# A third copy of VectorE's exponentials on GpSimd, split output projections, and zero products into a free bank

## The chip, the core and the metric

The kernel runs on one core of one Trainium2 chip. The metric is device time in microseconds, the median of the runs shown; times come with a trace of one profiled execution. The engines are named as in the profile: PE is TensorE (PEld its weight loads), ACT ScalarE, DVE VectorE, POOL GpSimd, SP the engine that issues DMAs.

## The reference

Four layers on a sequence of 2048 tokens of width 512, with 32 heads of 16. Layers 0 and 2 ("A") attend causally within segments of 512 tokens and add a memory term from the segments before; layers 1 and 3 ("B") are full attention over all 2048 tokens.

```python
def _A_ref(x, wq, wk, wv, wo, beta):              # H = 32, Dh = 16, N = 4 segments, L = 512
    ...
    for s in range(N):
        logits = einsum('bhqd,bhkd->bhqk', qs, ks) * scale + mask
        a_dot = einsum('bhqk,bhkd->bhqd', softmax(logits), vs)
        pq = phi(qs)                                # phi(t) = t + 1 where t > 0, else exp(t)
        a_mem = einsum('bhld,bhde->bhle', pq, M) / (einsum('bhld,bhd->bhl', pq, z)[..., None] + 1e-06)
        outs.append(g * a_mem + (1.0 - g) * a_dot)
        M = M + einsum('bhld,bhle->bhde', phi(ks), vs); z = z + phi(ks).sum(2)
    return o @ wo

def _B_ref(x, wqkv, wo):
    scores = einsum('bhqd,bhkd->bhqk', q, k) * Dh ** (-0.5)
    return einsum('bhqk,bhkd->bhqd', softmax(scores), v) @ wo

x = x + _A_ref(_layernorm(x), ...); x = x + _B_ref(_layernorm(x), ...)     # layers 0, 1
x = x + _A_ref(_layernorm(x), ...); x = x + _B_ref(_layernorm(x), ...)     # layers 2, 3
```

Most of the work is the exponentials of the scores: with 32 heads, each B layer alone has 32 x 2048 x 2048 of them.

## The kernel before

A planner in Python (`Builder`) writes out every engine's instruction list by hand. For each instruction it keeps an estimate of the engine's time (`self.sc.t[...]`, from the `ns` and `gap` that each call gives), and picks the next piece of work by these estimates. On the chip nothing is rearranged: each engine runs its list in order and waits on semaphores where a producer is another engine, or itself.

**Units.** Attention is worked in units (`unit`, L1322). A unit multiplies keys by masked queries (`qm`) into PSUM banks of 128 keys x 512 queries; four heads stand in four row tiles of TensorE, so a product takes 32 rows (`tile=(32, 32*r, 128, 0)`). Two bank groups take turns (`SLOTS`), three banks each; ScalarE then makes one exponential of 1024 or 1536 columns from two or three banks into `pT` (L1386). Two units later (`pv_step`, `pv`) TensorE multiplies values with `pT` into an accumulation bank, 17 columns a head: 16 of values and a column of ones for the softmax sum.

**VectorE's exponentials.** In B layers the planner may give chunks of 512 columns to VectorE (`dx_open`, `ring_open`, `dx_pick`). A chunk's scores go to a bank of their own (bank 3 or 7, `misc_bank` and `sums_bank`). VectorE computes scores times a constant plus a constant into 16-bit integers whose bits, read as bf16, are a straight-line approximation of the exponential: the first step, `dx_first`, L1022, from PSUM, for one chunk (512 columns) or a pair (1024). Then `task_dx` (L1043 to 1059) adds two constants (`EXP_STEPS`, 36 and 84) to these integers, SBUF to SBUF, 1024 columns each: two copies, L1054. TensorE sums the products of all three, which evens out the approximation, so each chunk costs three products with the values where ScalarE's costs one (`pv_taken`, `pv_phase`). A chunk's buffers are `dxt` at first; when layer 0 is done (`self.wide`) those of `KA`, `QA`, `VA` and of lent weights (`wA`, `wB`) are taken too, so the same line shows in the profile under several tiles.

**Between the units.** LayerNorm, projections, the memory, output projections and the copies are tasks, generators that yield `[needs], products on TensorE, ns on VectorE`; `background` and `bg_one` run them where the estimates have room. A task that yields `["cont"]` is in the middle of a product that holds `misc_bank`; while one is, no pair of chunks opens (L942) and the two special banks are not exchanged (`can_trade`). `task_out` (L844) is the output projection: four products with `wo` in a bank and an addition to the residual (L873), in one piece. `evac` (L450) moves a projection out of PSUM on VectorE, or on ScalarE where that engine's estimate is earlier by `EVAC_ACT`.

**Other work of GpSimd.** Causal masks in `pT` (L1400), masked queries (L1293) and ones in `VB` (L803). **Zero products.** `keep_busy` (L407) adds products with a zero matrix into the open accumulation bank when TensorE's recent share of streaming falls under `FILL`, to keep its clock up.

Of the kernel before, what the change touches and what calls it, by code (L numbers as in the profile page):

```python
# [12 lines left out]
NCH = 4  # L13
# [252 lines left out]
class Builder:  # L266
# [15 lines left out]
    PART = 2  # L282
    TRADE = 100
    BACK = 5
    FILL_DVE = 300
    EARLY = 200
    FILL = 0.48
    BUSY_ROOM, BUSY_BACK = 600, 1330
    BUSY_COLS = 1024
    DVE_FIN, DX_FIN = 600, 9000  # L290
    EVAC_ACT = 500
    DX_BANK, DX_LATE, BG_BANK, DVE_LATE, DVE_LATE_LOW = 500, 800, 200, 1200, 5000
    CR_A, CR_B, CR_W, CR_LOW, CARRY, CARRY_W, REST, NEAR, SLACK = 1450, 1500, 1700, 3000, 0, 800, 14, 14, 450
    ALT3, ALT5, GAP, AHEAD, PE_B, PE_A, PE_LOW, LOW, PAIRS, TAKEN, RATE, RATE_P = 2, 4, 2, 400, 4, 2, 5, 24, 30, 0.34, 1, 1
# [112 lines left out]
    def keep_busy(self):  # L407


        g = self.cur  # L410
        cols = 32 if g is not None and g.flip else 128
        while g is not None and g.npv and self.sc.t["pe"] + self.BUSY_ROOM < self.sc.t["act"] and self.bg_cols < self.BUSY_COLS and self.sc.streamed(
                max(self.sc.t["pe"], self.sc.t["act"] - self.BUSY_BACK), 3413) < self.FILL:
            bank = g.bank
            self.mm(self.ps[0:cols, bank.col0:bank.col0 + 512], self.zero[:, 0:cols], self.woB[:, 0, :], False, False,
                    [self.b_zero, self.b_woB], bank, g.acc, tile=(128, 0, cols, 0))
            self.bg_cols += 512
# [426 lines left out]
    def task_out(self, L, s):  # L844
        isA = L % 2 == 0
        wo, bwo = (self.woA, self.b_woA) if isA else (self.woB, self.b_woB)
        for ti in range(4):
# [3 lines left out]
            if isA and ti == 0:  # L851
# [11 lines left out]
                need.append(self.later())  # L863
            yield need, 4, 700
            t = 4 * s + ti
# [3 lines left out]
            srcs = [(self.oT[:, k, c, :], c, [self.b_oT[k][c]]) for c in range(NCH)]  # L869
            for n, (a, c, ba) in enumerate(srcs):  # L870
                self.bg_cols += 512
                self.mm_wide(bank, a[:, ti * 128:(ti + 1) * 128], wo[:, c, :], n == 0, n == len(srcs) - 1, list(ba) + [bwo], al)
# [170 lines left out]
    def task_dx(self):  # L1043
        while True:
            yield ["pair"], 0, 350
            b, ents = self.dx_pairs.pop(0)
            self.dx_now = ents
            w = 512 * len(ents)
            s = self.dx_buf(b, 0)[:, 0:w]
            for k, c in enumerate(EXP_STEPS):  # L1050
                if k:
                    yield [], 0, 350
                d = self.dx_buf(b, k + 1)[:, 0:w]
                self.op("dve", (lambda d, s, c: lambda e: e.tensor_scalar(d, s, float(c), None, op0=ALU.add))(d, s, c), reads=[self.b_dxt[b][0]],  # L1054
                        writes=[self.b_dxt[b][k + 1]], ns=430 if len(ents) == 2 else 295)
            self.dx_now = []
            self.dx_use[b] = len(ents)
            for i, (g, what, r) in enumerate(ents):
                self.dxq.append((self.step + self.DX_LAG, g, what, r, b, i, [0]))
# [499 lines left out]
    def pv_taken(self, g, now, used=()):  # L1559
# [5 lines left out]
        for ent in ents:  # L1565
            _, _, what, r, slot, i, done = ent
            while done[0] <= len(EXP_STEPS) and (now or not g.flip):
                self.pv_phase(ent)
        back = sum(len(EXP_STEPS) + 1 - ent[6][0] for ent in ents)
        for level in range(1, self.LEVEL + 1):  # L1570
            if level > 1 and max(loads) < level and back - self.BACK < 0:
                break
            for ent in ents:
                if ent[6][0] <= len(EXP_STEPS) and loads[ent[3]] < level:
                    loads[ent[3]] += 1
# [45 lines left out]
    def attention(self):  # L1621
# [19 lines left out]
        self.misc_banks = [self.misc_bank.idx]  # L1641
        self.unit_no = 0
        self.parts = {}
# [123 lines left out]
```

## Time and profile before

| | us |
|---|---|
| median of 3 runs | 1788.83 (1788.11, 1788.83, 1793.23) |
| profiled execution | 1788.65 |
| its span | 1786.7 |
| busy: ScalarE | 1729.1 |
| busy: TensorE, as matmuls | 1610.9 |
| busy: VectorE | 1504.3 |
| busy: GpSimd | 124.6 |

Busy time of an engine counts overlapping instructions once. The mean of one instruction is longer than its share, because an engine starts the next before the last has ended; the distance between starts is the price of one more. Matmuls are pipelined, so TensorE's busy time says little of its room. A window of the trace gives for each engine the busy time and, after x, the count of instructions.

### The profile page before, as it was taken

To read this page: it belongs to the slowest core of one execution; us is meant where nothing else is said; L and a number is where in the kernel's file an instruction comes from. 1 tells how busy PE (TensorE), PEld (TensorE's weight loads), DVE (VectorE), ACT (ScalarE), POOL (GpSimd) and SP (SyncE) were. 2 spreads that over 40 slices of the span, in tenths; PEclk is the share of its full clock that TensorE was granted. 3 is DMA by queue.
4 is the path that set the end of the run, shared out by engine and by line. 5 is a ranking of instruction groups with operands and counts; after the bars stand their busy time and mean duration, and the time that the engine had idled before them with its cause. 6 is when DMAs were issued, how large, how long until landed. Compare 5 with 4: busy or idle time off the path is not lost.

```text
span 1786.7 us, 45990 instructions
## 1 busy us (share of the span) xinstructions
PE 1610.9 (90%) x18926; PEld 578.7 (32%) x18995; DVE 1504.3 (84%) x3202; ACT 1729.1 (97%) x1613; POOL 124.6 (7%) x228
## 2 busy tenths in 40 slices
PE   8988898888998998899899999989899889889988
PEld 5542434222234222522235222432222222222225
DVE  5757666599995998699987999748999999999996
ACT  7999999999998999899999999999999999999998
POOL 1110101110001000100001000110100000000000
PEclk9999999999999999899999999999999999999999
DMA  5211211011101111101212111120100000000000
GB/s 172 34 23 28 37 22 25 14 27 49 25 11 29 51 40 34 33 15 46 63 18 36 46 37 33 20 55 8 31 13 19 10 12 24 10 10 17 16 13 18
DMA packets 148434, 54.50 MB, mean 31 GB/s; under 512 B 128768, under 2 KB 147712, under 8 KB 148224
## 3 DMA queue, kind: packets, MB, share of 16 engines
q1 hardware_dynamic: 148224, 51.56, 13.3%
q8 instruction: 149, 2.44, 0.6%
q14 instruction: 61, 0.50, 0.1%
HBM read 18.88 MB, written 2.10 MB: 12 GB/s over the span
## 4 chain that ended last, share of the span: by engine, by line
ACT 48%; PE 25%; issue 14%; DVE 12%; DMA 1%; POOL 0%; ACTq 0%; DVEq 0%; SPq 0%; POOLq 0%
ACT pT L1386 47%; PE ps L420 25%; DVE KA L1022 2%; DVE dxt L1022 1%; DVE dxt L1054 1%; ACT amem L650 1%; DVE VB L455 1%; DVE QA L1054 1%; DVE x L873 1%; DVE VA L1054 0%; DVE lnst L558 0%; DVE xn L585 0%; DVE wA L1022 0%; DVE qm L1293 0%; DVE oT L861 0%
## 5 line engine op out<-in xcount | busy, mean ns | idle before, releaser
L1386 ACT ACTIVATE pT<-ps 128x1024 bf16<-128x1024 f32 (+1 forms) x1572 | 1700.1, 1253 | 41.2 <-PE ps L420 37.0
L420 PE MATMUL ps<-qm,KB 32*128 32x512 bf16 x4096 | 582.4, 385 | 125.3 <-ACT pT L1386 106.3
L420 PE MATMUL ps<-pT,VB 128*17 128x512 bf16 x2961 | 505.0, 385 | 0.5 <-DVE x L873 0.2
L1022 DVE TENSOR_SCALAR KA<-ps 128x512 uint16<-128x512 f32 x549 | 381.2, 698 | 12.4 <-PE ps L420 8.0
L420 PEld LDWEIGHTS ps<-qm,KB 32*128 32x128 bf16 x4096 | 153.6, 91 | 645.4 <-ACT pT L1386 543.8
L1022 DVE TENSOR_SCALAR dxt<-ps 128x512 uint16<-128x512 f32 (+1 forms) x399 | 275.6, 692 | 7.4 <-PE ps L420 4.2
L420 PE MATMUL ps<-dxt,VB 128*17 128x512 bf16 x1179 | 278.6, 382 | 0.0
L420 PEld LDWEIGHTS ps<-pT,VB 128*17 128x17 bf16 x2961 | 118.2, 87 | 290.7 <-issue 279.6
L420 PE MATMUL ps<-QA,VB 128*17 128x512 bf16 x538 | 171.2, 382 | 0.0
L1054 DVE TENSOR_SCALAR dxt<-dxt 128x1024 uint16<-128x1024 uint16 (+1 forms) x414 | 164.1, 419 | 1.3
L420 PE MATMUL ps<-VA,VB 128*17 128x512 bf16 x538 | 158.1, 382 | 0.0
L420 PE MATMUL ps<-KA,VB 128*17 128x512 bf16 x538 | 145.1, 381 | 0.0
L1293 POOL TENSOR_SCALAR qm<-QB,par 128x512 bf16<-128x512 bf16 x90 | 68.3, 762 | 781.0 <-PE ps L420 745.1
L1054 DVE TENSOR_SCALAR QA<-KA 128x1024 uint16<-128x1024 uint16 (+1 forms) x284 | 120.5, 424 | 1.9
L1054 DVE TENSOR_SCALAR VA<-KA 128x1024 uint16<-128x1024 uint16 (+1 forms) x284 | 118.1, 416 | 0.0
L420 PE MATMUL ps<-qm,KA 32*128 32x128 bf16 (+2 forms) x1536 | 93.0, 257 | 18.9 <-ACT pT L1386 13.4
L420 PE MATMUL ps<-VA,pT 128*128 128x51 bf16 (+1 forms) x2560 | 106.6, 189 | 2.0 <-DVE ob L1481 1.3
L420 PE MATMUL ps<-woB,zero 128*32 128x512 bf16 (+1 forms) x306 | 101.4, 383 | 0.2
L1400 POOL TENSOR_SCALAR_AFFINE_SELECT pT<-pT 128x256 bf16<-128x256 bf16 (+4 forms) x92 | 48.7, 544 | 748.5 <-ACT pT L1386 694.2
L420 PEld LDWEIGHTS ps<-VA,pT 128*128 128x128 bf16 x2560 | 92.6, 97 | 19.8 <-issue 8.5
L420 PE MATMUL ps<-xT,wB 128*32 128x512 bf16 (+1 forms) x747 | 74.6, 381 | 2.2 <-DVE VA L1054 0.5
L420 PE MATMUL ps<-xT,wA 128*32 128x512 bf16 (+1 forms) x524 | 68.5, 381 | 4.4 <-DMA xT<-xn 1.3
(138 smaller groups left out, 1421.3 us busy)
## 6 DMA issues: line engine op xcount, KB each, us to landing
wB<-in_B_wqkv_dram SPq DMA_DIRECT2D x48, 128.0 KB, 2.3
wA<-in_A_wk_dram SPq DMA_DIRECT2D x16, 128.0 KB, 2.2
wA<-in_A_wq_dram SPq DMA_DIRECT2D x16, 128.0 KB, 2.3
wA<-in_A_wv_dram SPq DMA_DIRECT2D x16, 128.0 KB, 2.4
out_dram<-x SPq DMA_DIRECT2D x8, 256.0 KB, 2.2
x<-in_A_x_dram SPq DMA_DIRECT2D x3, 512.0 KB, 8.1
wB<-in_B_wqkv_dram SPq DMA_DIRECT2D x1, 1536.0 KB, 11.6
oT<-ob SPq DMA_TRANSPOSE x63, 2.5
```

Source lines behind the costliest of these rows:

```text
L420: self.sc.add("pe", lambda e: e.matmul(out, lhsT, rhs, start=start, stop=stop, skip_group_check=True), reads=reads, banks=[(bank, "w", all ...
L455: self.op("dve", lambda e: e.tensor_copy(dst, src), writes=bdst, bank=bank, alloc=al, ns=690)
L650: self.op("act", lambda e: e.activation(et, src, ACT.Exp), reads=bsrc, writes=self.b_amem, ns=1023, gap=915)
L873: self.op("dve", (lambda t, o: lambda e: e.tensor_tensor(self.x[:, t, :], self.x[:, t, :], o, ALU.add))(t, o), reads=[self.b_x[t]], writes ...
L1022: self.op("dve", lambda e: e.tensor_scalar(d, o, SCALE * LOG2E * 128, 127.0 * 128 + EXP_BIAS, op0=ALU.mult, op1=ALU.add), writes=[self.b_d ...
L1054: self.op("dve", (lambda d, s, c: lambda e: e.tensor_scalar(d, s, float(c), None, op0=ALU.add))(d, s, c), reads=[self.b_dxt[b][0]], writes ...
L1293: self.op(eng, (lambda m, q, col: lambda e: e.tensor_scalar(m, q, col, 0.0, op0=ALU.mult, op1=ALU.add))(m, q, col), reads=[bq, self.b_par] ...
L1386: self.sc.add("act", (lambda dst, src: lambda e: e.activation(dst, src, ACT.Exp, scale=SCALE))(dst, src), writes=self.b_pT[slot * 3 + i:sl ...
L1400: self.op("pool", (lambda blk, pat: lambda e: e.affine_select(blk, blk, pattern=pat, compare_op=ALU.is_ge, fill=0.0, base=0, channel_multi ...
```

## The change

Four things, and constants that go with them. (1) In `task_dx`, where a chunk pair is full (1024 columns), the kernel is in its wide stage, GpSimd's estimated time is under VectorE's by the measure `POOL_COPY` and neither chunk's group is near its end, the copy with 84 goes to GpSimd, ahead of VectorE's copy with 36; both read the first step's output. (2) `pv_taken` leaves out a chunk's next product while the copy that it reads is not estimated to be ready within `DX_READY`. (3) `task_out` in the wide stage yields after its first product (four instructions) and goes on with the other three. (4) `keep_busy`, where no accumulation is open, may write zero products into the special bank that comes free first.

```diff
+    POOL_COPY, POOL_NEAR, DX_READY = 1000, 10, 300
+    OPART = 1
...
-    BUSY_ROOM, BUSY_BACK = 600, 1330
+    BUSY_ROOM, BUSY_BACK = 400, 1330
     BUSY_COLS = 1024
+    BUSY_WAIT = 200
     DVE_FIN, DX_FIN = 600, 9000
-    EVAC_ACT = 500
-    DX_BANK, DX_LATE, BG_BANK, DVE_LATE, DVE_LATE_LOW = 500, 800, 200, 1200, 5000
-    CR_A, CR_B, CR_W, CR_LOW, CARRY, CARRY_W, REST, NEAR, SLACK = 1450, 1500, 1700, 3000, 0, 800, 14, 14, 450
+    EVAC_ACT = 300
+    DX_BANK, DX_LATE, BG_BANK, DVE_LATE, DVE_LATE_LOW = 500, 900, 200, 1200, 5000
+    CR_A, CR_B, CR_W, CR_LOW, CARRY, CARRY_W, REST, NEAR, SLACK = 1450, 1500, 1700, 3000, 0, 800, 12, 12, 450
     ALT3, ALT5, GAP, AHEAD, PE_B, PE_A, PE_LOW, LOW, PAIRS, TAKEN, RATE, RATE_P = 2, 4, 2, 400, 4, 2, 5, 24, 30, 0.34, 1, 1
     NKS, DX_LAG = 6, 2
     DMA_STEPS, DMA_LATE = 1, 300
@@ -408,12 +411,18 @@
 
 
         g = self.cur
-        cols = 32 if g is not None and g.flip else 128
-        while g is not None and g.npv and self.sc.t["pe"] + self.BUSY_ROOM < self.sc.t["act"] and self.bg_cols < self.BUSY_COLS and self.sc.streamed(
+        bank, al = (g.bank, g.acc) if g is not None and g.npv else (None, None)
+        while self.sc.t["pe"] + self.BUSY_ROOM < self.sc.t["act"] and self.bg_cols < self.BUSY_COLS and self.sc.streamed(
                 max(self.sc.t["pe"], self.sc.t["act"] - self.BUSY_BACK), 3413) < self.FILL:
-            bank = g.bank
-            self.mm(self.ps[0:cols, bank.col0:bank.col0 + 512], self.zero[:, 0:cols], self.woB[:, 0, :], False, False,
-                    [self.b_zero, self.b_woB], bank, g.acc, tile=(128, 0, cols, 0))
+            if al is None:
+                g = self.pvq[0][1] if self.pvq else None
+                half = any(t["next"][0][:1] == ["cont"] for t in self.tasks) or self.parts
+                bank = min([self.sums_bank] if half else [self.sums_bank, self.misc_bank], key=self.wait_of)
+                if g is None or self.wait_of(bank) > self.sc.t["pe"] + self.BUSY_WAIT:
+                    return
+            cols = 32 if g.flip else 128
+            self.mm(self.ps[0:cols, bank.col0:bank.col0 + 512], self.zero[:, 0:cols], self.woB[:, 0, :], al is None, al is None,
+                    [self.b_zero, self.b_woB], bank, self.new_alloc() if al is None else al, tile=(128, 0, cols, 0))
             self.bg_cols += 512
 
     def mm(self, out, lhsT, rhs, start, stop, reads, bank, alloc, name="", tile=(128, 0, 128, 0), n=512):
@@ -861,13 +870,16 @@
                     self.op("dve", (lambda o, m, gc: lambda e: e.scalar_tensor_tensor(o, o, gc, m, op0=ALU.mult, op1=ALU.add))(o, m, gc),
                             reads=[self.b_gfm, self.b_phq[c], self.b_oT[0][c]], writes=[self.b_oT[0][c]], ns=690)
                 need.append(self.later())
-            yield need, 4, 700
+            half = self.wide and self.OPART < NCH
+            yield need, self.OPART if half else 4, 0 if half else 700
             t = 4 * s + ti
             bank, al = self.misc(), self.new_alloc()
             o = self.ps[:, bank.col0:bank.col0 + 512]
             k = L % 2
             srcs = [(self.oT[:, k, c, :], c, [self.b_oT[k][c]]) for c in range(NCH)]
             for n, (a, c, ba) in enumerate(srcs):
+                if half and n == self.OPART:
+                    yield ["cont"], NCH - n, 700
                 self.bg_cols += 512
                 self.mm_wide(bank, a[:, ti * 128:(ti + 1) * 128], wo[:, c, :], n == 0, n == len(srcs) - 1, list(ba) + [bwo], al)
             self.op("dve", (lambda t, o: lambda e: e.tensor_tensor(self.x[:, t, :], self.x[:, t, :], o, ALU.add))(t, o),
@@ -1047,10 +1059,17 @@
             self.dx_now = ents
             w = 512 * len(ents)
             s = self.dx_buf(b, 0)[:, 0:w]
-            for k, c in enumerate(EXP_STEPS):
-                if k:
+            share = len(ents) == 2 and self.wide and self.POOL_COPY and self.sc.t["pool"] < self.sc.t["dve"] + self.POOL_COPY and not any(
+                len(g.banks) - g.pos < self.POOL_NEAR for g, _, _ in ents)
+            for k, c in sorted(enumerate(EXP_STEPS), reverse=share):
+                if k == (0 if share else 1):
                     yield [], 0, 350
                 d = self.dx_buf(b, k + 1)[:, 0:w]
+                if share and k:
+                    self.op("pool", (lambda d, s, c: lambda e: e.tensor_scalar(d, s, float(c), None, op0=ALU.add))(d, s, c), reads=[self.b_dxt[b][0]],
+                            writes=[self.b_dxt[b][k + 1]], ns=1400, gap=1350)
+                    self.copies += 1
+                    continue
                 self.op("dve", (lambda d, s, c: lambda e: e.tensor_scalar(d, s, float(c), None, op0=ALU.add))(d, s, c), reads=[self.b_dxt[b][0]],
                         writes=[self.b_dxt[b][k + 1]], ns=430 if len(ents) == 2 else 295)
             self.dx_now = []
@@ -1567,11 +1586,12 @@
             while done[0] <= len(EXP_STEPS) and (now or not g.flip):
                 self.pv_phase(ent)
         back = sum(len(EXP_STEPS) + 1 - ent[6][0] for ent in ents)
+        ready = lambda ent: self.b_dxt[ent[4]][ent[6][0]].last_write.end + LAG["dve"] <= self.sc.t["pe"] + self.DX_READY
         for level in range(1, self.LEVEL + 1):
             if level > 1 and max(loads) < level and back - self.BACK < 0:
                 break
             for ent in ents:
-                if ent[6][0] <= len(EXP_STEPS) and loads[ent[3]] < level:
+                if ent[6][0] <= len(EXP_STEPS) and loads[ent[3]] < level and ready(ent):
                     loads[ent[3]] += 1
                     back -= 1
                     self.pv_phase(ent)
@@ -1639,7 +1659,7 @@
         self.step = self.bg_cols = 0
         self.misc_bank, self.sums_bank = self.banks[MISC], self.banks[SUMS]
         self.misc_banks = [self.misc_bank.idx]
-        self.unit_no = 0
+        self.unit_no = self.copies = 0
         self.parts = {}
         self.make_groups()
         self.make_tasks()
```

The built programs hold, before and after: exponentials on ScalarE of 1024 columns 1023 and 1078, of 1536 columns 549 and 480, of 512 none and 1; first steps on VectorE of one chunk 1001 and 1017, of a pair 21 and 61; copies of 1024 columns on VectorE 1026 and 588, on GpSimd none and 536; zero products 314 and 288; evacuations of projections and of sums on ScalarE (L453) 7 and 13.

## The prediction

> **What bounds the kernel now.** I read the page's head, then the waits, then the windows of 100 us.
>
> ```profile
> span 1786.7 us, 45990 instructions
> PE 1610.9 (90%) x18926; PEld 578.7 (32%) x18995; DVE 1504.3 (84%) x3202; ACT 1729.1 (97%) x1613; POOL 124.6 (7%) x228
> ...
> ACT 48%; PE 25%; issue 14%; DVE 12%; DMA 1%; POOL 0%; ACTq 0%; DVEq 0%; SPq 0%; POOLq 0%
> ```
>
> ScalarE is busy for 97% of the span and leads the chain. The waits say who is waited for:
>
> ```profile
> PEld ps L420 <- ACT pT L1386: 581.0, 1202, 1.2
> ...
> ACT pT L1386 <- PE ps L420: 37.0, 68, 3.1
> ...
> PEld ps L420 <- DVE KA L1022: 20.7, 52, 0.9
> ```
>
> TensorE waits 581 us for exponentials to free a bank; ScalarE waits 37 us for TensorE. The windows (PE, PEld, DVE, ACT and POOL busy, clock, DMA) show a second engine at its limit:
>
> ```profile
> 400.00:500.00 100.00, 90.40 (x909) 24.32 (x908) 97.47 (x207) 99.86 (x101) 0.75 (x1) 1.00 0.15 35
> 500.00:600.00 100.00, 88.82 (x1215) 38.76 (x1217) 77.70 (x169) 94.52 (x88) 8.30 (x14) 0.97 0.13 26
> 700.00:800.00 100.00, 92.18 (x1199) 40.13 (x1207) 79.24 (x167) 92.46 (x83) 11.87 (x25) 0.95 0.11 21
> 800.00:900.00 100.00, 91.03 (x915) 25.34 (x911) 96.44 (x213) 99.79 (x99) 0.00 (x0) 1.00 0.22 53
> 1000.00:1100.00 100.00, 90.77 (x909) 25.61 (x906) 97.29 (x212) 99.26 (x98) 4.03 (x7) 1.00 0.17 41
> 1300.00:1700.00 400.00, 364.79 (x3534) 97.44 (x3534) 391.30 (x798) 399.74 (x415) 14.63 (x18) 1.00 0.07 15
> 400.00:1700.00 1300.00, 1183.64 (x12984) 381.20 (x13011) 1169.43 (x2445) 1275.09 (x1231) 72.78 (x123) 0.99 0.13 28
> ```
>
> In full windows ScalarE stands at 99 to 100% and VectorE at 96 to 98%; elsewhere VectorE has room (78, 79%). From 400 to 1700 VectorE idles 1300 - 1169 = 131 us. So the softmax work is shared between two full engines, and a cheaper share on VectorE buys time only where VectorE really gets free.
>
> **ScalarE's saving.** I counted instructions in the two built programs; the retuned constants act through these counts alone. Exponentials of 1024 columns go from 1023 to 1078, of 1536 from 549 to 480, and one of 512 appears; VectorE takes 1139 chunks of 512 columns in place of 1043. Six evacuations move to ScalarE.
>
> ```profile
> 1353.63 16.63 ACT L1386 ACTIVATE pT<-ps 128x1024 bf16<-128x1024 f32 x18
> 234.07 21.64 ACT L1386 ACTIVATE pT<-ps 128x1536 bf16<-128x1536 f32 x16
> L1386 ACT ACTIVATE pT<-ps 128x1024 bf16<-128x1024 f32 x1023 | 974.1, 1120 | 4.0 <-PE ps L420 2.5 <-ACT pT L1386 0.2
> L1386 ACT ACTIVATE pT<-ps 128x1536 bf16<-128x1536 f32 x549 | 782.0, 1502 | 37.2 <-PE ps L420 34.5
> L453 ACT ACTIVATE VA<-ps 128x512 bf16<-128x512 f32 x3 | 1.8, 599 | 1.3 <-PE ps L420 1.1
> ```
>
> Unbroken runs give the pitch: (16.63 - 1.12) / 17 = 0.912 us and (21.64 - 1.50) / 15 = 1.343 us, shorter than one instruction because neighbours overlap. So +55 x 0.912 = +50.2, -69 x 1.343 = -92.7, and the 512 and the six evacuations, at about 0.5 each, +3.5: **-39 us**, if ScalarE stays as full as before.
>
> **VectorE's load.** Timeline rows of VectorE and GpSimd:
>
> ```profile
> 1277.67 0.42 DVE L1054 TENSOR_SCALAR VA<-KA 128x1024 uint16<-128x1024 uint16 x1
> 1278.00 0.69 DVE L1022 TENSOR_SCALAR KA<-ps 128x512 uint16<-128x512 f32 x1
> 1278.60 0.83 DVE L1054 TENSOR_SCALAR QA<-KA 128x1024 uint16<-128x1024 uint16 x1
> 1279.36 0.41 DVE L1054 TENSOR_SCALAR VA<-KA 128x1024 uint16<-128x1024 uint16 x1
> ...
> 1278.46 0.69 POOL L1293 TENSOR_SCALAR qm<-QB,par 128x512 bf16<-128x512 bf16 x1 [3.91 <-PE ps L420]
> ...
> 363.10 0.43 DVE L1054 TENSOR_SCALAR dxt<-dxt 128x1024 uint16<-128x1024 uint16 x1
> 363.17 0.92 POOL L1293 TENSOR_SCALAR qm<-QB,par 128x512 bf16<-128x512 bf16 x1 [6.08 <-PE ps L420]
> ...
> L1022 DVE TENSOR_SCALAR KA<-ps 128x1024 uint16<-128x1024 f32 x13 | 15.9, 1222 | 3.1 <-PE ps L420 3.0
> ```
>
> Starts give a pitch of 0.33 for a copy and 0.60 for a chunk's first step (L1022); the pair form, 1.222 long, has about 1.14. Counted: copies of 1024 fall from 1026 to 588, first steps of 512 rise from 1001 to 1017, pair forms from 21 to 61. So -438 x 0.33 = -144.5, +16 x 0.60 = +9.6, +40 x 1.14 = +45.6: -89.
>
> The same rows show the price. The copy at 1278.60 took 0.83, not 0.42: it stood until GpSimd ended at 1279.15. At 363.10 the copy came first and kept 0.43; GpSimd took 0.92 and ended 0.56 after it. The eviction from PSUM beside it was not stretched. So a copy on VectorE and an operation on GpSimd exclude each other, and the first one delays the other.
>
> ```profile
> 1284.53 0.69 DVE L1022 TENSOR_SCALAR KA<-ps 128x512 uint16<-128x512 f32 x1
> 1285.24 0.43 DVE L1054 TENSOR_SCALAR QA<-KA 128x1024 uint16<-128x1024 uint16 x1
> ...
> 127.40 0.69 DVE L455 CAST QB<-ps 128x512 bf16<-128x512 f32 x1 [1.68 <-PE ps L420]
> 128.19 1.36 POOL L1293 TENSOR_SCALAR qm<-QB,par 128x512 bf16<-128x512 bf16 x2 [4.34 <-DVE QB L455]
> ...
> L1293 POOL TENSOR_SCALAR qm<-QB,par x90: 686/692/1194, 128.2 to 1654.4; 128x512 bf16<-128x512 bf16 x90
> ...
> L1400 POOL TENSOR_SCALAR_AFFINE_SELECT pT<-pT 128x512 bf16<-128x512 bf16 x23 | 14.9, 646 | 170.3 <-ACT pT L1386 170.3
> L1400 POOL TENSOR_SCALAR_AFFINE_SELECT pT<-pT 128x768 bf16<-128x768 bf16 x13 | 11.3, 869 | 43.0 <-ACT pT L1386 43.0
> ```
>
> VectorE goes on 0.02 us after its own step; GpSimd starts 0.10 us after VectorE's. So where the remaining copy stands right behind the first step, VectorE wins and GpSimd waits. GpSimd's 1024 columns are not in the trace: 256 more columns cost 0.223 us, so 512 more cost 0.446, and 0.692 + 0.446 = **1.14 us**. Bounds: 0.869 + 0.223 = 1.09 below, 1.194 + 0.446 = 1.64 above. I take 1.14, nearest to the median of the same operation. The Trainium skill, GPSIMD Engine Reference, section Performance versus the Vector engine, gives 1.03 cycles an element, at 1.2 GHz, where the loop body has at most two operations, and about 1.8 as the best of a longer one. By the first, 512 more columns cost 0.44 us, as the slope here (0.87 ns an element) has it; by the second, as an estimate, 0.77, the copy takes 1.46 us and the waits below sum to about 200 us.
>
> Of the 536 shared copies in the built program, 355 have VectorE's copy right behind the first step. Then GpSimd ends 0.56 + 0.446 = 1.0 us behind that copy, and 56 of these meet another VectorE operation of this kind sooner, at about 0.64: 36 us. Where one other instruction lies between (99), the copy comes 0.6 after the step but GpSimd holds until 0.10 + 1.14 = 1.24: 0.65 each, 64 us. Two between (49): 0.1, 5 us. None, but another SBUF operation first (10): 1.2, 12 us. Sum **118 us** of waits; with 1.09 it is 108, with 1.64 it is 272.
>
> **Where it lands.**
>
> ```profile
> L1400 POOL TENSOR_SCALAR_AFFINE_SELECT pT<-pT x92: 292/520/957, 15.7 to 1163.1; 128x256 bf16<-128x256 bf16 x26, 128x512 bf16<-128x512 bf16 x23, 128x128 bf16<-128x128 bf16 x17, 128x384 bf16<-128x384 bf16 x13
> ```
>
> GpSimd's masks end at 1163 us; behind that only attention is left. There stand 272 shared copies but 38 us of waits, against -50 us of VectorE work: VectorE gets lighter, and ScalarE's share there (-26 of 1536 columns, +17 of 1024) gives -19.5 us in full. Before that, waits are 80 and VectorE's work falls by 41: +39 net.
>
> ```profile
> 400.00:500.00 100.00, 57.23 (x82) 1.00 0.15 35
> 800.00:900.00 100.00, 52.76 (x77) 1.00 0.22 53
> 1000.00:1100.00 100.00, 51.49 (x76) 1.00 0.17 41
> 400.00:1200.00 800.00, 320.29 (x465) 0.99 0.16 36
> ```
>
> These windows of first steps alone (L1022) put 235 of 465 into the three full ones. There VectorE gets about +20 against 2.5 + 3.6 + 2.7 = 8.8 us of idle time: 11 us longer. The other half has room and gains half of ScalarE's other 19.5, -10. Total -19.5 + 11 - 10 = **-18.5 us**.
>
> **Edits at nothing.** The +175 products on TensorE lie under its 581 us of waiting; bare they are at most 175 x 0.385 = 67 us.
>
> ```profile
> L420 PE MATMUL ps<-pT,VB 128*17 128x512 bf16 x2961 | 505.0, 385 | 0.5 <-DVE x L873 0.2
> ```
>
> Splitting output projections adds no instruction; while one is half done no pair may open and TensorE's bank stays taken, and the counts above hold what that displaces. On GpSimd the masks and query masks now queue behind copies of up to 1.4 us; GpSimd is at 7%, and the products that need them come two units later, so 0, and 1.4 us each where that lead is used up. The readiness test puts late copies' products later in TensorE's queue; without it the next scores would queue behind GpSimd's 1.14 us. Zero products go from 314 to 288, into a free bank too: the clock shows 0.97 and 0.95 in two windows, so 8 us either way; I take 0.
>
> The profiled execution took 1788.65 us against the span's 1786.7, and the median is 1788.83: 1788.65 - 18.5 = **1770 us**. Own range 1760 to 1782. About 0.3% (5 us) is what a measurement can tell.
>
> **Rivals.** (a) Full gain: the planner's other slots swallow the waits, 1788.65 - 39 = 1750. For it: ScalarE holds 399.74 of 400 us beside 14.63 us of GpSimd work. Against: VectorE at 97%. Chance 0.16. (b) Slower by VectorE's waits: TensorE's queue is in order, so a chunk bank freed 0.65 us late holds the next scores, and ScalarE has only two slots. If all 80 us before 1163 pass on, 1788.65 - 39 + 80 = 1830 (1868 with all 118). It decides once over a third, 39 of 118, passes. For it: TensorE's waits for L1022 exist. Against: they sum to 20.7 and are 0.9 at most. Chance 0.20. (c) GpSimd's copy is slower than the slope says. At 1.64 us the waits of 272 make VectorE's load +183, which is 91 more than its 131 of idle time less the 39 of shortening: 1750 + 91 = 1841. For it: no row has this shape or this type on GpSimd. Against: masks and the query mask lie on one slope. The page's second figure, with its 1.46 us, points to this side. Chance 0.06. (d) Nothing moves: the waits eat just the gain, 1788. Chance 0.08.
>
> **How the numbers follow.** The forecast has 0.50. Faster: 0.50 + 0.16 and the lighter edge of (d), 0.67; same 0.10; slower 0.23. The range 1747 to 1815 leaves out (c) and the upper half of (b), under 0.2.
>
> **What would show it.** GpSimd copies of 1.14 us alone and about 1.4 when VectorE goes first; VectorE copies in two groups, 0.42 and about 1.1, the second near 110 to 175 times; full windows before 1163 at VectorE 99% with ScalarE below 99%; behind it ScalarE at 99 to 100% and some 20 us shorter. It is wrong if VectorE's copies right behind a first step wait, or if GpSimd's copies pass 1.6 us.

## The result and the profile after

The changed kernel takes 2190.72 us (median of 4 runs, 2189.35 to 2192.89) against 1790.74 (4 runs, 1788.11 to 1793.23): ratio 1.2235 [1.221, 1.226], 22% slower. The forecast was 1770, its range 1747 to 1815. The head of the page after, with the chain's shares by engine:

```profile
span 2190.2 us, 47358 instructions
PE 1823.9 (83%) x19170; PEld 598.7 (27%) x19170; DVE 1625.4 (74%) x2808; ACT 1739.3 (79%) x1606; POOL 1651.1 (75%) x783
...
POOL 34%; PE 25%; issue 20%; DVE 10%; ACT 9%; DMA 0%; SPq 0%; POOLq 0%; ACTq 0%; DVEq 0%
```

GpSimd went from 124.6 us of work to 1651.1 and leads the chain that ScalarE led with 48%. The instructions on its copy's line, with their shortest, median and longest duration in ns, say why (48 more copies stand on `wA` and `wB`):

```profile
L1069 POOL TENSOR_SCALAR VA<-KA x289: 2762/2792/3322, 317.5 to 2173.4; 128x1024 uint16<-128x1024 uint16 x145
L1069 POOL TENSOR_SCALAR dxt<-dxt x199: 2762/2808/3220, 314.7 to 2176.1; 128x1024 uint16<-128x1024 uint16 x199
```

Not one copy takes less than 2.76 us; 1.14 was forecast, with 1.64 as the upper bound. All 536 at their median of 2.80 are 1500 us, where the planner had charged GpSimd 1.35 us for each. The waits of after:

```profile
ACT pT L1405 <- PE ps L429: 421.9, 451, 5.7
PEld ps L429 <- ACT pT L1405: 366.7, 723, 1.6
...
PEld ps L429 <- POOL VA L1069: 193.3, 152, 5.4
PE ps L429 <- POOL VA L1069: 139.1, 121, 5.1
...
PEld ps L429 <- POOL dxt L1069: 99.7, 83, 3.7
PE ps L429 <- POOL dxt L1069: 69.5, 61, 3.2
```

TensorE, whose list is in order, stands in the last four rows before products that need GpSimd's copy, up to 5.4 us at a time. The rows sum to 502 us; weight loads (PEld) and matmuls (PE) often wait at the same time, and with such overlaps counted once it is 293 us. The next scores are queued behind them, so ScalarE waits 421.9 us for TensorE where it waited 37.0. The windows (PE, PEld, DVE, ACT and POOL busy, clock, DMA):

```profile
400.00:500.00 100.00, 75.14 (x629) 18.20 (x633) 73.60 (x115) 68.86 (x70) 97.62 (x39) 0.86 0.13 27
800.00:900.00 100.00, 85.80 (x966) 32.23 (x963) 83.36 (x152) 83.15 (x77) 72.44 (x34) 0.93 0.14 33
1600.00:1700.00 100.00, 74.13 (x566) 16.37 (x564) 73.14 (x103) 66.95 (x68) 100.00 (x40) 0.81 0.03 6
1200.00:2100.00 900.00, 725.15 (x6321) 185.88 (x6321) 666.76 (x1043) 666.68 (x642) 805.13 (x338) 0.84 0.08 16
```

Where only B work is left (1600 to 1700) GpSimd is full and ScalarE, at 399.74 of 400 us there before, is at 67%. The granted clock of TensorE is 0.993 over the whole run before and 0.895 after; of the windows of 100 us shown, it is lowest, 0.81, where GpSimd is full. How much of the loss the lower clock added, no run separates.

### The profile page after: what moved, and what is told of

Same layout as the page of the kernel before. It is cut to its first block, busy times and chain, and to the rows that moved or that the text cites. A ratio compares the mean times of both kernels' runs of the same rounds, so it can differ in the third digit from the quotient of the medians.

```text
span 2190.2 us, 47358 instructions
## 1 busy us (share of the span) xinstructions
PE 1823.9 (83%) x19170; PEld 598.7 (27%) x19170; DVE 1625.4 (74%) x2808; ACT 1739.3 (79%) x1606; POOL 1651.1 (75%) x783
## 4 chain that ended last, share of the span: by engine, by line
POOL 34%; PE 25%; issue 20%; DVE 10%; ACT 9%; DMA 0%; SPq 0%; POOLq 0%; ACTq 0%; DVEq 0%
PE ps L429 25%; POOL VA L1069 18%; POOL dxt L1069 11%; ACT pT L1405 9%; POOL wA L1069 2%; DVE KA L1034 2%; DVE dxt L1034 2%; POOL wB L1069 1%; POOL qm L1312 1%; DVE lnst L567 1%; DVE dxt L1073 1%; DVE xn L594 1%; DVE VB L464 0%; ACT amem L659 0%; DVE QA L1073 0%
## 5 line engine op out<-in xcount | busy, mean ns | idle before, releaser
L1405 ACT ACTIVATE pT<-ps 128x1024 bf16<-128x1024 f32 (+1 forms) x1559 | 1707.0, 1167 | 432.8 <-PE ps L429 421.9
L1069 POOL TENSOR_SCALAR VA<-KA 128x1024 uint16<-128x1024 uint16 x289 | 822.1, 2858 | 73.6 <-DVE KA L1034 68.2
L429 PE MATMUL ps<-qm,KB 32*128 32x512 bf16 x4096 | 634.5, 425 | 92.9 <-ACT pT L1405 56.2
L1069 POOL TENSOR_SCALAR dxt<-dxt 128x1024 uint16<-128x1024 uint16 x199 | 569.6, 2868 | 81.1 <-DVE dxt L1034 49.8
L429 PE MATMUL ps<-pT,VB 128*17 128x512 bf16 x2867 | 544.9, 419 | 0.1
L1034 DVE TENSOR_SCALAR KA<-ps 128x512 uint16<-128x512 f32 (+1 forms) x572 | 406.1, 713 | 137.5 <-PE ps L429 127.2
L429 PE MATMUL ps<-dxt,VB 128*17 128x512 bf16 x1281 | 332.6, 427 | 68.0 <-POOL dxt L1069 67.3
L429 PE MATMUL ps<-VA,VB 128*17 128x512 bf16 x577 | 194.0, 438 | 135.4 <-POOL VA L1069 134.9
L1419 POOL TENSOR_SCALAR_AFFINE_SELECT pT<-pT 128x256 bf16<-128x256 bf16 (+4 forms) x109 | 58.1, 548 | 306.5 <-ACT pT L1405 306.4
L1073 DVE TENSOR_SCALAR QA<-KA 128x1024 uint16<-128x1024 uint16 (+1 forms) x305 | 208.5, 685 | 6.3
L429 PE MATMUL ps<-QA,VB 128*17 128x512 bf16 x577 | 206.4, 434 | 0.3
L429 PEld LDWEIGHTS ps<-dxt,VB 128*17 128x17 bf16 x1281 | 63.8, 89 | 100.1 <-POOL dxt L1069 97.0
```

The costliest lines, as they stand in the source:

```text
L429: self.sc.add("pe", lambda e: e.matmul(out, lhsT, rhs, start=start, stop=stop, skip_group_check=True), reads=reads, banks=[(bank, "w", all ...
L1034: self.op("dve", lambda e: e.tensor_scalar(d, o, SCALE * LOG2E * 128, 127.0 * 128 + EXP_BIAS, op0=ALU.mult, op1=ALU.add), writes=[self.b_d ...
L1069: self.op("pool", (lambda d, s, c: lambda e: e.tensor_scalar(d, s, float(c), None, op0=ALU.add))(d, s, c), reads=[self.b_dxt[b][0]], write ...
L1405: self.sc.add("act", (lambda dst, src: lambda e: e.activation(dst, src, ACT.Exp, scale=SCALE))(dst, src), writes=self.b_pT[slot * 3 + i:sl ...
L1419: self.op("pool", (lambda blk, pat: lambda e: e.affine_select(blk, blk, pattern=pat, compare_op=ALU.is_ge, fill=0.0, base=0, channel_multi ...
```

## The experiments

"Before" below is the kernel before, timed beside each kernel. "VectorE's waits" is worked out from the trace alone: of each line and shape on VectorE, what instructions take beyond the tenth percentile of their group, where that is over 60 ns. It is 11.5 us in the kernel before and 184.6 in the one after.

**What the copy costs by itself.** The kernel before, with GpSimd instructions put at its start while VectorE is idle.

```diff
+for _ in range(2):                                                          # u: uint16, f: bf16, 128 x 1024
+    one(lambda e: e.tensor_scalar(u[1], u[0], 84.0, None, op0=ALU.add))                # L502
+    ...
+    one(lambda e: e.tensor_scalar(f[1], f[0], 84.0, None, op0=ALU.add))                # L504
+    ...
+    one(lambda e: e.tensor_scalar(f[1], f[0], 1.0, 0.0, op0=ALU.mult, op1=ALU.add))    # L506
+    ...
```

> The kernel before, with eighteen GpSimd operations put at its start, where VectorE has nothing to do yet; they work on idle buffers and change no result, but delay the start by some 30 us. It measures the disputed operation by itself. Own-time theory (GpSimd is slow on 16-bit integers as such): the addition on 1024 uint16 columns takes 2.76 us with VectorE idle, on 512 about 1.5, on 1024 bf16 columns 1.14. Port theory (VectorE's copies keep GpSimd off the memory): all of them take 1.14 us at 1024 columns here, 0.69 at 512. An integer addition of pairs, 512 int32 columns with two inputs, is measured beside them: about 0.7 us if it goes one column a cycle, about 1.3 if two inputs share one port.

The timeline of GpSimd in that kernel (start, duration):

```profile
6.26 2.78 POOL L502 TENSOR_SCALAR dxt<-dxt 128x1024 uint16<-128x1024 uint16 x1
9.13 1.49 POOL L503 TENSOR_SCALAR dxt<-dxt 128x512 uint16<-128x512 uint16 x1
10.70 2.77 POOL L504 TENSOR_SCALAR dxt<-dxt 128x1024 bf16<-128x1024 bf16 x1
...
15.12 1.05 POOL L506 TENSOR_SCALAR dxt<-dxt 128x1024 bf16<-128x1024 bf16 x1
...
23.30 1.04 POOL L510 TENSOR_TENSOR dxt<-dxt,c 128x512 int32<-128x512 int32 x1
```

VectorE has no instruction in this stretch, and the copy takes 2.78 us: waiting for VectorE has no part in it. The fast row (L506) differs from the slow one of the same type (L504) in its operations: multiply and add, as in the query mask, against add alone. The number type makes no difference to the addition (2.78 and 2.77). A second set of instructions went after what the form decides:

```diff
+    one(lambda e: e.tensor_scalar(u[1], u[0], 1.0, 84.0, op0=ALU.mult, op1=ALU.add))    # L502
+    one(lambda e: e.tensor_scalar(f[1], f[0], 1.0, None, op0=ALU.mult))                 # L503
+    one(lambda e: e.tensor_scalar(u[1], u[0], 42.0, 42.0, op0=ALU.add, op1=ALU.add))    # L504
+    one(lambda e: e.tensor_scalar(u[1], u[0], 84.0, 0.0, op0=ALU.add, op1=ALU.max))     # L505
+    one(lambda e: e.tensor_scalar(u[1], u[0], 84.0, 1.0, op0=ALU.add, op1=ALU.mult))    # L506
+    ...
```

> Again the kernel before with GpSimd operations on idle buffers at its start, each twice. Form theory (GpSimd takes some 2.5 ns a column when the instruction has one operation, and 0.8 when it has a multiplication and an addition): on 1024 uint16 columns, multiply by 1 and add 84 takes 1.05 us; multiply alone in bf16 takes 2.77 as add alone did. Type theory: uint16 is slow in either form and multiply-add on it takes 2.77. Open is what add-add, add-max and add-multiply take, and a plain copy: if only a leading multiplication is fast they take 2.77, if any two operations are, 1.05.

```profile
6.27 1.04 POOL L502 TENSOR_SCALAR dxt<-dxt 128x1024 uint16<-128x1024 uint16 x1
7.40 2.79 POOL L503 TENSOR_SCALAR dxt<-dxt 128x1024 bf16<-128x1024 bf16 x1
10.27 3.65 POOL L504 TENSOR_SCALAR dxt<-dxt 128x1024 uint16<-128x1024 uint16 x1
14.01 3.63 POOL L505 TENSOR_SCALAR dxt<-dxt 128x1024 uint16<-128x1024 uint16 x1
17.72 1.04 POOL L506 TENSOR_SCALAR dxt<-dxt 128x1024 uint16<-128x1024 uint16 x1
18.85 0.62 POOL L507 TENSOR_SCALAR dxt<-dxt 128x512 uint16<-128x512 uint16 x1
19.53 1.04 POOL L508 COPY dxt<-dxt 128x1024 uint16<-128x1024 uint16 x1
```

At 1024 columns multiply with add, in either order, takes 1.04 us, as does a plain copy; one operation alone takes 2.77 to 2.79; add and add, or add and maximum, 3.63 to 3.65. So more operations are not slower as such. Why these pairs are fast no run shows.

**The other edits.** Everything of the change stays but the sharing.

```diff
-    POOL_COPY, POOL_NEAR, DX_READY = 1000, 10, 300
+    POOL_COPY, POOL_NEAR, DX_READY = 0, 10, 300
```

> The changed kernel without the shared copy (the planner never gives one to GpSimd); split projections, readiness test, zero products and constants stay. Own-time and port theory: the loss sits in the shared copy, so the time is within 1% of before, 1775 to 1805. Rival (the other edits cost it): it stays over 1900.

1793.46 us, ratio 1.0018 [1.0007, 1.003]: the split, the readiness test, the zero products and the constants cost 3 us together. So practically all of the 400 us come with the shared copy.

**Another type.**

```diff
-... e.tensor_scalar(d, s, float(c), None, op0=ALU.add) ...
+... e.tensor_scalar(d.bitcast(dt.bfloat16), s.bitcast(dt.bfloat16), 1.0, None, op0=ALU.mult) ...
```

> The changed kernel, same plan and same order, but GpSimd's operation is typed bf16 and multiplies by 1, so the constant 84 is not added there: it leaves out that part of the computation. Buffers, sizes and waits are the same. Own-time theory: GpSimd needs 1.14 us for it and the time falls to what was forecast for that price, 1750 to 1815. Port theory: GpSimd still takes about 2.8 us and the time stays near 2190.

2192.01 us, ratio 1.2239 [1.2217, 1.2261]. The theory of a slow integer type fell; a multiplication alone is as slow as an addition alone.

**The true price in the planner.**

```diff
-                            writes=[self.b_dxt[b][k + 1]], ns=1400, gap=1350)
+                            writes=[self.b_dxt[b][k + 1]], ns=2850, gap=2770)
```

> The changed kernel with the planner told 2.85 us for GpSimd's copy in place of 1.40. Own-time theory: the plan then gives GpSimd only what it can do, some 350 to 450 copies in place of 536, TensorE's waits for GpSimd (502 us) nearly go, and the time is 1770 to 1860. Port theory: VectorE's copies still lose to GpSimd's holding of the port, fewer chunks fit, and the time stays over 1900.

1969.34 us, ratio 1.1011 [1.0979, 1.1043], outside the 1770 to 1860 expected for a GpSimd that is only slow, and over the 1900 given for VectorE's waits. Chain and ScalarE's wait in this kernel:

```profile
DVE 36%; PE 34%; ACT 13%; issue 12%; POOL 4%; DMA 1%; DVEq 0%; ACTq 0%; SPq 0%; POOLq 0%
...
ACT pT L1405 <- PE ps L429: 190.5, 336, 2.7
```

340 copies are shared now and GpSimd is 57% busy, so it keeps up: TensorE's waits for GpSimd, over all rows, fall from 562 us to 21 (from 330 to 17 with overlaps counted once). But VectorE waits 216.5 us and leads the chain. So the long operation does harm in two ways: as a queue on GpSimd that runs late, and through VectorE, which GpSimd holds up. That the first is worth the step from 1969 to 2191, and the second the step from before to 1969, is an estimate from the traces: the planner's lists differ as well.

**The fast form.** The same constant added, by the pair that the probes found.

```diff
-... e.tensor_scalar(d, s, float(c), None, op0=ALU.add) ...
+... e.tensor_scalar(d, s, 1.0, float(c), op0=ALU.mult, op1=ALU.add) ...
```

> The changed kernel, same plan and same order, with GpSimd's copy written as multiply by 1, add 84, on uint16; its result is the same number. Form theory: 1.05 us alone and about 1.35 behind a VectorE copy, and the time is the one that was forecast for a price of 1.14, near 1770 (1750 to 1815). Port theory: VectorE's waits, forecast at 118 us, pass on and the time lies over 1794, up to 1868. Type theory: near 2190 still.

1829.46 us, ratio 1.0205 [1.0182, 1.0227]. VectorE and GpSimd side by side in this kernel's timeline:

```profile
1454.42 0.43 DVE L1073 TENSOR_SCALAR dxt<-dxt 128x1024 uint16<-128x1024 uint16 x1
...
1454.47 1.28 POOL L1069 TENSOR_SCALAR dxt<-dxt 128x1024 uint16<-128x1024 uint16 x1 [2.28 <-PE ps L429]
...
L1069 POOL TENSOR_SCALAR VA<-KA x289: 1047/1281/1303, 318.5 to 1804.2; 128x1024 uint16<-128x1024 uint16 x145
...
ACT pT L1405 <- PE ps L429: 88.4, 193, 1.8
...
1300.00:1600.00 300.00, 281.02 (x2628) 77.29 (x2624) 287.96 (x480) 288.99 (x301) 187.11 (x161) 0.99 0.08 17
```

Of the 536 copies 313 take 1.28 us: VectorE's copy began first, kept its 0.43 and GpSimd waited, as forecast (355, 1.4 us). The other VectorE copies pay: 141 of 588 wait 0.52 us on average, and all of VectorE's waits come to 104.4 us. TensorE never stands before one of GpSimd's copies here: of the rows of its waits for GpSimd none names one. But the time did not land at the forecast 1770; it landed at rival (b)'s 1830, and from 1300 to 1600, where the full gain was forecast, ScalarE is at 96%.

**The same by another instruction**, pairs of 16-bit numbers added as 32-bit integers (1.04 us alone, the last row of the first probe).

```diff
-... e.tensor_scalar(d, s, float(c), None, op0=ALU.add) ...
+... e.tensor_tensor(d.bitcast(dt.int32), s.bitcast(dt.int32), bcast(self.c32[:, 0:1], [[0, 512]]), ALU.add) ...
```

> The changed kernel with GpSimd's copy written as an integer addition on 512 int32 columns, which adds 84 to both 16-bit halves at once, against a constant of one column; exact. Measured alone before it took 1.04 us. Form theory: about the same time as multiply-add, 1750 to 1815. If a GpSimd instruction with two inputs holds VectorE longer, VectorE's copies wait longer than with multiply-add and the time is 10 to 40 us above it.

1825.98 us, ratio 1.0186 [1.017, 1.0202], VectorE's waits 100.4: the price decides, not the instruction.

**A dose on fixed lists.** Every instruction of the fast form stays where it is; only the width of GpSimd's operation changes; the kernel leaves out the rest of that copy.

```diff
-... e.tensor_scalar(d, s, 1.0, float(c), op0=ALU.mult, op1=ALU.add) ...
+... e.tensor_scalar(d[:, 0:64], s[:, 0:64], 1.0, float(c), op0=ALU.mult, op1=ALU.add) ...      # or 0:512
```

> The kernel with multiply-add on GpSimd, same plan and order, but GpSimd's operation covers 64 of its 1024 columns; the rest of that copy is left out of the computation. Port theory (VectorE's waits of 93 us for GpSimd are what lifts that kernel to 1829): the waits go and the time falls to the forecast's floor, 1745 to 1770. Rival (the plan with 96 more chunks costs it by itself, on TensorE or in banks): it stays over 1800.

> The instruction lists of two_op and of tiny, GpSimd's operation on 512 of the 1024 columns (0.62 us alone in the measured prices, against 1.05 for 1024 and 0.24 for 64); the other half of the third copy is stale. Port theory: the waits fall faster than the operation's length, since a VectorE copy that comes 0.6 us after the first step then finds the operation over: waits of 15 to 40 us, time 1765 to 1790. Rival (GpSimd's late results, not VectorE's waits, hold TensorE): in proportion to the length, half of the way from 1756 to 1829, 1793 or more, whatever the waits.

64 columns: 1756.47 us, ratio 0.9805 [0.9786, 0.9823]. 512 columns: 1769.04, ratio 0.9872 [0.9849, 0.9895]. The row of ScalarE's wait and the window 1300 to 1600 with 64 columns, then the same with 512:

```profile
ACT pT L1405 <- PE ps L429: 35.9, 83, 1.8
...
1300.00:1600.00 300.00, 276.85 (x2753) 71.43 (x2752) 284.53 (x495) 299.23 (x317) 75.18 (x170) 1.00 0.07 15
```

```profile
ACT pT L1405 <- PE ps L429: 45.7, 103, 1.9
...
1300.00:1600.00 300.00, 278.97 (x2723) 74.47 (x2722) 285.49 (x491) 297.50 (x315) 133.25 (x170) 1.00 0.07 15
```

On one list the width gives waits of 8.8, 30.7 and 104.4 us and times of 1756, 1769 and 1829: 0.6 us of time for one of waiting over the first step, 0.8 over the second. With the waits gone ScalarE is full again (299.23 of 300) and the whole gain is there. Half the columns bring far less than half of the loss, which speaks against late results of GpSimd as the cause, as does the fast form's trace, in which no product waits for one. What VectorE meets at 512 columns is an operation that is mostly over when its next copy comes.

**Can the waits be avoided?** Four attempts with the full, fast operation. First, GpSimd made to stand behind VectorE's own copy, and the fast price in the planner:

```diff
-            for k, c in sorted(enumerate(EXP_STEPS), reverse=share):
-                if k == (0 if share else 1):
+            for k, c in enumerate(EXP_STEPS):
+                if k and not share:
...
-                            reads=[self.b_dxt[b][0]], writes=[self.b_dxt[b][k + 1]], ns=1400, gap=1350)
+                            reads=[self.b_dxt[b][0], self.b_dxt[b][1]], writes=[self.b_dxt[b][k + 1]], ns=1150, gap=1080)
```

> Multiply-add on GpSimd, and GpSimd's copy is made to wait for VectorE's copy of the same pair, with both planned together and GpSimd's at its measured price (1.15 us); so GpSimd can never be first. Port theory: VectorE's waits fall from 93 us to under 45 (what is left are operations that come within 1.1 us behind the pair), and the time to 1765 to 1800. Rival: the waits only move to the next operation, and the time stays at 1815 to 1835.

1803.56 us, ratio 1.0072 [1.0049, 1.0095]; waits 64.0: better than 1829, but short of the 1765 to 1800 and the 45 us expected. Then the planner was told the rule that the two exclude each other, with this order (first) and with the change's own (second):

```diff
+            end = max(self.t[e] + gap, ready + ns)
+            if e == "dve" and port:                       # VectorE's operations within SBUF
+                for a, b in self.hold:                    # GpSimd's operations: (start, end)
+                    if a + 70 < end - ns < b:
+                        end = b + ns - 140
+                ...
```

> As the kernel before it in this batch, and the planner's estimate knows the rule: a VectorE operation of the blocked kinds that would start while GpSimd works is put behind it. Port theory: the plan gives fewer chunks away where VectorE is held, and nothing queues behind a wait that was not planned: 1755 to 1790, at or under the kernel without the rule. Rival: the plan's errors are not what costs; within 5 us of it.

> The changed kernel's own order (GpSimd's copy planned first) with multiply-add, its measured price and the same rule in the planner. If unplanned waits are the cost, it falls from 1829 to 1790 to 1815; if the waits cost as such, planned or not, it stays within 10 us of 1829.

1799.46 us, ratio 1.0045 [1.0022, 1.0068], and 1804.48, ratio 1.0073 [1.0046, 1.01]. The first is within 5 us of the kernel without the rule, as its rival had it; the second came down into the range given for unplanned waits, 1790 to 1815. Knowing the waits, the planner gives VectorE less: ScalarE's list is only 6 and 17 us shorter than before, and the waits stay at 74.8 and 107.8.

Third, fewer collisions, on top of the first attempt: a copy is shared only where no second pair is queued behind, and, in the second kernel, only once layer 2's memory is done ("last layers" below).

```diff
-            share = ... self.wide and self.POOL_COPY and ...
+            share = ... self.wide and self.POOL_COPY and not self.dx_pairs and ...
+            share = ... self.POOL_COPY and ("mem", 2, 3) in self.flags and not self.dx_pairs and ...    # the second
```

> As the run behind (GpSimd adds with the two-operation form and stands behind VectorE's own copy), but a copy is shared only where no second pair of chunks is queued behind it: 442 shared copies instead of 487, and in the program 93 of them have another SBUF operation of VectorE close behind instead of 144. Port theory (what is left of the loss is VectorE waiting for GpSimd's operations, and most of a wait passes to ScalarE): waits of about 35 us against 64 in behind and 11.5 before, ScalarE 31 us shorter than before, time 1775 to 1792. Rival (the planner's new arrangement of the work itself costs the time, whatever the waits): as behind, 1798 to 1808, with the waits about halved.

> As v_nopair, but copies are shared only after layer 2's memory is done, where GpSimd has hardly any other work and the windows of before showed VectorE at 98%: 242 shared copies, 56 with another SBUF operation of VectorE close behind; ScalarE's instructions sum to 20.5 us less than before. Port theory: waits of about 22 us, time 1775 to 1788, faster than the kernel before. Rival (the arrangement costs the time): 1790 or more, and the stretch from 1300 to 1700 us no shorter than before.

1800.44 us, ratio 1.0058 [1.0044, 1.0071], and 1790.26, ratio 0.9998 [0.9989, 1.0007]. The waits fell to 41.9 and 30.2, yet neither kernel got below before: both came out at the rival's figures. Whether the waits that are left or the new arrangement of the work cost the time, the same two lists with 64 columns tell:

> The instruction lists of v_nopair, but GpSimd's operation covers 64 of the 1024 columns, so the third product of those chunks sums stale columns. Port theory: VectorE's waits fall to about 10 us and the time by what they cost, to the 31 us that ScalarE's list is shorter: 1760 to 1768. Rival (this arrangement of the work costs the time): 1790 or more, as v_nopair with 1800.

> The instruction lists of v_late_nopair, GpSimd's operation on 64 of 1024 columns, so the third product of those chunks sums stale columns. Port theory: 20.5 us below the kernel before, 1768 to 1776. Rival (arrangement): 1785 to 1792, as v_late_nopair with 1790.

1774.74 us, ratio 0.9915 [0.9898, 0.9931], and 1779.39, ratio 0.9932 [0.9914, 0.9949], between what the two theories gave. Both have a part: the arrangement loses 16 and 10 us of the gains of 31 and 20.5, the operation's width 26 and 11.

Fourth, the fast copy in two instructions of 512 columns, so that VectorE can come in between (the second kernel also with the restriction of the third attempt):

```diff
+                    for h in range(2):
+                        self.op("pool", (...)(d[:, 512 * h:512 * h + 512], s[:, 512 * h:512 * h + 512], c),
+                                reads=[self.b_dxt[b][0]], writes=[self.b_dxt[b][k + 1]], ns=700, gap=675)
```

> As two_op, but GpSimd adds 84 in two instructions of 512 columns (0.62 us each alone), so that VectorE can come in between; 528 shared copies, ScalarE's instructions sum to 38 us less than before. Theory (the length of one GpSimd operation sets VectorE's wait): a VectorE copy 0.6 us after the first step waits 0.1 us, not 0.65; waits of 30 to 60 us against 104 in two_op, and at the 0.6 to 0.8 us of time per us of wait seen from tiny over half to two_op, 1768 to 1790, faster than before. Rival (each half takes its own wait, and GpSimd holds for 1.24 us in all): waits of 100 us or more and 1825 or more.

> As halves, but a copy is shared only where no second pair of chunks is queued behind it: 438 shared copies, ScalarE 33 us shorter. Theory: waits of 20 to 40 us, and some 10 us lost by the arrangement as in v_nopair_tiny: 1770 to 1788. Rival: as v_nopair, 1798 or more.

1793.55 us, ratio 1.0012 [1.0003, 1.0021], and 1801.09, ratio 1.0051 [1.0036, 1.0066]. Two halves hold GpSimd longer than one whole (0.62 us each alone, against 1.04), but VectorE's waits fall from 104.4 to 69.6 and 36 us come back: the length of one operation counts for more than their sum. Both figures lie above the 30 to 60 us of waits and the 1768 to 1790 us expected, and it doesn't beat before. The second kernel comes out in its rival's range, 1798 or more, with waits of 59.5.

The kernels with the multiply-add, by what they save in ScalarE's list (counted in the built programs with the prediction's 0.912 and 1.343 us for each exponential, and about half a microsecond for each evacuation that moves to ScalarE) and what they lose. "Loss" is the difference of time plus the saving:

| kernel | ScalarE's list | VectorE's waits over before | time against before | loss |
|---|---|---|---|---|
| 64 columns | -39.6 | -2.7 | -36.2 | 3 |
| 512 columns | -39.6 | 19.2 | -21.1 | 19 |
| 1024 columns | -39.6 | 92.9 | +36.7 | 76 |
| two halves | -38.0 | 58.1 | +2.3 | 40 |
| behind VectorE's copy | -35.9 | 52.5 | +10.9 | 47 |
| two halves, no second pair | -32.9 | 48.0 | +9.9 | 43 |
| no second pair | -31.1 | 30.4 | +9.9 | 41 |
| same, 64 columns | -31.1 | -3.5 | -15.4 | 16 |
| last layers | -20.5 | 18.7 | -0.3 | 20 |
| same, 64 columns | -20.5 | 1.4 | -10.7 | 10 |
| rule in the planner, behind | -6.0 | 63.3 | +6.8 | 13 |
| rule in the planner, change's order | -17.3 | 96.3 | +11.8 | 29 |

Three lists were also run with 64 columns, and there nothing but GpSimd's width differs: 0.6 to 0.8 us of time is lost for each us of wait. In the other rows the loss holds the arrangement as well. Where the planner knows of the waits the whole loss is a fifth to a third of them, but it then leaves ScalarE its work. Why two of the arrangements lose 10 to 16 us without waits is open.

## Why the prediction was wrong

**The step that failed is the price of GpSimd's copy.** The sum took 1.14 us, "nearest to the median of the same operation", from the query mask with 0.446 us more for 512 columns. It measured 2.77. The row was of the same opcode and the slope was sound: multiply-add of 1024 columns takes 1.05. But the query mask is a multiply-add and the copy an add, which the profile doesn't tell apart: both are a TENSOR_SCALAR there. The upper bound of 1.64 fell with it, because it was a longest instance of that other operation. The Trainium skill's page that the prediction drew on, GPSIMD Engine Reference, Performance versus the Vector engine, gives 1.03 cycles an element for at most two operations. The multiply-add agrees: 512 more columns cost 0.42 us (0.62 to 1.04) against the 0.44 estimated from that figure; the single addition does not, with 1.29 (1.49 to 2.78). The estimate of 1.46 us from the Trainium skill's slower figure was also too low. Rival (c), "GpSimd copy is slower", is what happened, at a price beyond its end and by two mechanisms in place of one: not VectorE's waits alone (216.5 us with the true price planned) but GpSimd as a queue that runs late (330 us of TensorE's waits, overlaps counted once). Its chance of 0.06 was far too low where, as it said itself, no row had the operation. The signal named, copies over 1.6 us, came.

**With the price mended, the second step fails: how much of the waits passes on.** The fast form is the kernel that the prediction thought of. Its waits were sized well: 118 us forecast (its four terms sum to 117), 92.9 over before measured; copies at 1.28 us against 1.4; VectorE first in 313 cases against 355. They also lie about when they were forecast: 34 us behind 1163 us against 38, and 59 ahead of it against 80. But the time is +36.7 against the forecast -18.5. Behind 1163 us the full gain was to come, since VectorE's load falls there. The window 1300 to 1600 of the kernel before is

```profile
1300.00:1600.00 300.00, 273.35 (x2640) 72.63 (x2640) 294.06 (x603) 299.91 (x312) 12.55 (x15) 1.00 0.07 15
```

In the fast form VectorE's load does fall there, to 287.96, and yet ScalarE has 288.99 of 300: 11 us are missing, with 17 us of VectorE's waits in that window. So VectorE's total load is not what passes on. A VectorE result is late by half a microsecond at one place, and TensorE's queue hands it on: its waits for the first steps on `KA` rise from 20.7 us before, in the weight-load row, to

```profile
PEld ps L429 <- DVE KA L1034: 47.8, 104, 1.7
```

in the fast form. Over all first steps and both kinds of row, overlaps counted once (worked out from the traces), these waits are 42 us before, 102 in the fast form and 32 with 64 columns: the 70 between the last two are about the 73 us by which the time differs. The argument against rival (b), that such waits sum to 20.7 and are 0.9 at most, was true of before and is what the change altered. (b) asked over a third of the waits to pass; with the loss of 76 for 92.9 it is about four fifths.

**What held.** ScalarE's saving of 39 us: with 64 columns its busy time falls by 35.2 and the time by 36.2, to 1756.47, close to rival (a)'s 1750. VectorE's lighter load: -89 was forecast, the same kernel's busy time shows

```profile
PE 1605.1 (92%) x19170; PEld 570.7 (33%) x19170; DVE 1441.5 (82%) x2808; ACT 1693.9 (97%) x1606; POOL 339.3 (19%) x783
```

1504.3 - 1441.5 = 63, in the forecast direction and some 26 less. The rule of exclusion, and who wins it, held for the fast form. And the edits put at nothing cost 3 us together.

## What to carry to other kernels

Price an operation on GpSimd by a row with the same arithmetic, not just the same opcode and shape, and where there is none let the range be wide: here multiply-add took 1.04 us and add 2.77 at 128x1024. Work moved to GpSimd beside a VectorE that copies within SBUF was paid for here in waits; in an in-order pipeline with few buffers like this one, count most of each wait as lost, whatever the mean load says, and try several short operations in place of one long one. To find what such a move costs, keep every instruction and shrink the suspected one to a few columns: the difference of the two times is what its length costs on that list. Another arrangement of the work has a floor of its own, as the rows with 64 columns show.

## What the runs showed of the hardware

Two things were not expected: that the pair of arithmetic operations sets GpSimd's time (above), and that the slow form doesn't hold VectorE off for its whole length. In the kernel after, VectorE's and GpSimd's rows:

```profile
853.94 2.77 POOL L1069 TENSOR_SCALAR VA<-KA 128x1024 uint16<-128x1024 uint16 x1
...
855.01 0.42 DVE L1073 TENSOR_SCALAR wA<-wA 128x1024 uint16<-128x1024 uint16 x1
855.35 0.42 DVE L1073 TENSOR_SCALAR QA<-KA 128x1024 uint16<-128x1024 uint16 x1
...
1497.72 2.77 POOL L1069 TENSOR_SCALAR VA<-KA 128x1024 uint16<-128x1024 uint16 x1
...
1497.76 1.28 DVE L1073 TENSOR_SCALAR QA<-KA 128x1024 uint16<-128x1024 uint16 x1
...
1499.67 1.10 DVE L1073 TENSOR_SCALAR QA<-KA 128x1024 uint16<-128x1024 uint16 x1
```

The copy 0.04 us into GpSimd's operation ends 1.32 us into it, that is 0.28 us after 1.04, the length of the whole fast form; the one 1.95 us in ends 0.28 us after GpSimd does; the two at 1.07 and 1.41 us wait for nothing. Beside GpSimd's copies of under 2.80 us, all 49 of VectorE's 1024-column copies that start 0.9 to 1.5 us in go free, and none of the 67 that start 1.7 to 2.6 us in. So the slow form holds VectorE off twice, not throughout. That it goes over the data in two passes would fit, but no run tests it.
